# A delta-rule chain between two feed-forward layers: one tiling for K S and Q S, and a fixed place for each step of a chunk

## The chip, the cores and the metric

The kernel runs on one core of a Trainium2 chip. The metric is the device time of one execution in microseconds. A core has five engines, each with an instruction queue of its own that it works through in order: TensorE (PE, with its weight loads as PEld), VectorE (DVE), ScalarE (ACT), GpSimd (POOL) and SyncE (SP), which here issues the DMAs. They meet only through semaphores.

## The reference

A recurrence over 768 tokens for 32 pairs of batch and head (state 48 x 48), then two feed-forward layers over the 3072 tokens, 384 to 2048 to 384 each, all in float32:

```python
for t in range(S):
    kt, vt, bt = (k_n[:, :, t], v[:, :, t], beta[:, :, t, None])
    y[:, :, t] = np.einsum('bhd,bhde->bhe', q[:, :, t], state)
    v_old = np.einsum('bhde,bhd->bhe', state, kt)
    state = state + bt[:, :, :, None] * np.einsum('bhd,bhe->bhde', kt, vt - v_old)
...
g = np.where(pos, h, np.where(neg, 0.0, (h + beta) ** 2 / (4.0 * beta)))   # layer 1, h = x @ w_in
...
r = np.maximum(h, 0.0); g = r * r                                            # layer 2
```

Here k_n is k divided by its norm. Each layer ends with g @ w_out.

## The kernel before

**Chunks.** The 768 tokens are cut into 24 chunks of 32 tokens. A chunk has the 4 batches x 32 tokens on 128 partitions and the 8 heads side by side. For chunk c the steps are, all as short matmuls on tiles of TensorE's array: `ks` (K S and Q S from the state `st` into the two tiles `yo`, line 507; L516 on VectorE, twice, makes the residual `r` from it), `tr` (the triangular inverse times the residual, line 521, copied out by L529 on ScalarE), `ku` (K'U, line 556, into two tiles `sps`; four additions L568 on VectorE bring it into the state), `pu` (P U added to Q S in `yo`, line 538; L546 on ScalarE and L547 on VectorE write y) and `xt` (three transposes, line 585; L587 on ScalarE and L588 on VectorE split the result into `xh` and `xl`, the input of the first feed-forward layer). The state makes `ks` of a chunk wait for `ku` of the one before.

**Tiles of K S.** `kqt` holds k and q of a chunk side by side (2 x 32 columns). For chunks from 4 on, the loads swap k and q for odd batches, so one matmul of 64 columns puts K S and Q S of every batch where they belong. Chunks 2 and 3 (0 and 1 don't use the state) are loaded unswapped: there a matmul of 64 columns serves the even batches and two of 32 columns the odd ones, in turn. The profile shows each float32 matmul as two.

**Grams and solves.** `gram(c)` makes the products of a chunk's k and q (line 301, masked by L317). The chunks stand in groups (2, 4, 4, 4, 4, 4, 2); for each group one triangular solve `tri` turns the grams into inverses: L371 transposes on VectorE, some small steps lead up to L410, 30 pairs of L431 and L432 run on GpSimd, and L435 transposes back on VectorE. GpSimd also scales each chunk's v (L277).

**Feed-forward.** The tokens go through layer 1 in nine blocks of 2 or 3 chunks (SIZES 2, 2, 3, 3, 3, 3, 3, 2, 3), then through layer 2 in eight of 3 chunks. A block takes 16 iterations f. In iteration x TensorE does `hidden` (h, 9 matmuls, line 602) and, two iterations late, `out1` or `out2` (acc, 9 matmuls, line 602). Between them ScalarE and VectorE work in turn: L628, L629, L630, L631, L639, L640 in layer 1. Weights for layer 2 are converted on the way (L186, L189, L195).

**Order.** TensorE's order is the program's; that of the other engines comes from a scheduler. An iteration has two slots: slot 2x stands behind `hidden`, slot 2x+1 behind the output products. A block has 32 slots. Block n's chunks run in the slots of block n-1 (those of block 1 from slot 19 on). Before, the five steps of a block's chunks, with the grams of the next group put between the steps of one chunk, stood in one list that was spread evenly over the slots. `ready` and `at`, the slots of grams and of `ks`, set when the solves begin and end: L371 one slot after the group's last gram, L435 one slot ahead of the `ks` of the group's first chunk.

Of the kernel before, what the change touches and what calls it, by code (L numbers as in the profile page):

```python
# [19 lines left out]
SIZES = [2, 2, 3, 3, 3, 3, 3, 2, 3]  # L20

GROUPS = [2, 4, 4, 4, 4, 4, 2]
# [3 lines left out]
def kernel(  # L26
# [25 lines left out]
    B, H, T = 4, 8, 32  # L52
# [16 lines left out]
    KQ, KG = 4, 2  # L69
# [3 lines left out]
    HEAD = 19  # L73
# [214 lines left out]
    def gram(c, lo=0, hi=2, late=0, eng=None):  # L288


        n, j = group_of[c]
        if j == 0 and lo == 0:
            gp[n] = ring.tile([P, 2, GC, H, T], F32, tag="gp", bufs=2, name="gp")
            if GROUPS[n] < GC:
                nc.gpsimd.memset(gp[n][:, 0, GROUPS[n]:], 0.0)
        g = att([P, H, hi - lo, T], "g")
        src = kqt[c] if c < KQ else kqg[c]

        def one_(b, h, p, pd):
            x = src[pd, b // 2, h]  # L300
            nc.tensor.matmul(  # L301
                g[p, h].rearrange("p x i -> p (x i)"), x[:, 0:T], x[:, lo * T:hi * T],
                start=h == 0, stop=True, skip_group_check=True,
            )

        per_bh(one_)
        if c >= KQ:
            kqg.pop(c)
            if late < 2:
                load_kg(c + KG)  # L310

        dst = gp[n][:, lo:hi, j].rearrange("p x h i -> p h x i")
        if late > 1:
            nc.scalar.copy(dst, g)

        def keep():
            (eng or nc.vector).tensor_mul(  # L317
                dst,
                dst if late > 1 else g,
                mask[:, lo:hi].rearrange("p (o x) i -> p o x i", o=1)  # L320
                .to_broadcast([P, H, hi - lo, T]),
            )

        if late:
            return keep
        keep()
# [151 lines left out]
    def chunk_steps(c):  # L478
        n, j = block_of[c]
        g, gj = group_of[c]  # L480
        t = {}

        def of_heads(o, x):

            for a in range(c):
                per_bh(lambda b, h, p, pd: nc.tensor.matmul(
                    o[p, h], cross[a, c][p, h, x], us[a][p, h],
                    start=a == 0 and h == 0, stop=x == 0 and a == c - 1,
                    skip_group_check=True,
                ))  # L490

        def ks():
            r = t["r"] = kvt[c][:, 1]
            if 0 < c < HEADS:
                o = att([P, H, D], "ks")
                of_heads(o, 0)
                nc.vector.tensor_sub(r, r, o)
            elif c:
                o = t["o"] = [ps.tile([P, H, D], F32, tag=f"yo{x}", name="yo") for x in range(2)]

                def one_(b, h, p, pd):
                    x = kqt[c][pd, b // 2, h]
                    rows = [(x, 64 * (b // 2), 64)]
                    if b % 2 and c < KQ:
                        rows = [(x[:, 0:T], T * b, T), (x[:, T:2 * T], T * (b - 1), T)]
                    for x, q, w in rows:
                        nc.tensor.matmul(  # L507
                            o[b % 2][q:q + w, h], x, st[pd, b // 2, h],
                            start=h == 0, stop=False, skip_group_check=True,
                        )  # L510

                per_bh(one_)
                kqt.pop(c)
                load_kq(c + KQ)
                for x in range(2):
                    nc.vector.scalar_tensor_tensor(  # L516
                        r, o[x], side[:, 2 * x:2 * x + 1], r, ALU.mult, ALU.add)

        def tr():
            o = att([P, H, D], "tr")  # L520
            per_bh(lambda b, h, p, pd: nc.tensor.matmul(  # L521
                o[p, h], gp[g][p, 0, gj, h], t["r"][p, h],
                start=h == 0, stop=True, skip_group_check=True,
            ))
            if c >= HEADS:
                us[c] = t["r"]
            else:
                us[c] = wp.tile([P, H, D], F32, tag=spare[f"u{c}"], name="u")
            nc.scalar.copy(us[c], o)  # L529

        def qs():
            o = t["o"] = att([P, H, D], "yy")
            of_heads(o, 1)

        def pu():
            o = t["o"]
            y = t["y"] = t["r"]
            per_bh(lambda b, h, p, pd: nc.tensor.matmul(  # L538
                o[p, h] if c < HEADS else o[b % 2][T * (b ^ 1):T * (b ^ 1) + T, h],
                gp[g][p, 1, gj, h], us[c][p, h],  # L540
                start=c == 0 and h == 0, stop=True, skip_group_check=True,
            ))
            if c < HEADS:
                nc.scalar.copy(y, o)
            else:
                nc.scalar.mul(y, o[0], side[:, 1:2])  # L546
                nc.vector.scalar_tensor_tensor(y, o[1], side[:, 3:4], y, ALU.mult, ALU.add)  # L547

        def ku():
            k_ = kvt[c]  # L550
            if c < NCH - 1:
                kf = k_.rearrange("p x h d -> p (x h d)")
                w = 64 if c == 0 else D
                if c not in range(1, HEADS):
                    s_ps[:] = [att([P, H, D], "sps") for x in range(B2)]
                per_bh(lambda b, h, p, pd: nc.tensor.matmul(  # L556
                    s_ps[b // 2][pd.start:pd.start + w, h], kf[p, D * h:D * h + w], us[c][p, h],
                    start=c not in range(1, HEADS) and h == 0, stop=c >= HEADS - 1,
                    skip_group_check=True,
                ))  # L560
                if c == HEADS - 1:
                    nc.vector.tensor_copy(st[:, 0], s_ps[0])
                    nc.scalar.copy(st[:, 1], s_ps[1])
                elif c >= HEADS:
                    for x in range(B2):
                        for o in range(2):
                            d = st[64 * o:64 * o + D, x]
                            nc.vector.tensor_add(d, d, s_ps[x][64 * o:64 * o + D])  # L568
            done()

        def done():

            t["n"] = t.get("n", 0) + 1
            if t["n"] == 2:
                del kvt[c]
                load_kv(c + 3)

        def xt():
            if j == 0:
                xh[n] = ring.tile([P, KT, P * SIZES[n]], F32R, tag="xh", bufs=2, name="xh")  # L580
                xl[n] = ring.tile([P, KT, P * SIZES[n]], F32R, tag="xl", bufs=2, name="xl")
            o = att([P, KT, P], "xt")
            yf = t["y"].rearrange("p h d -> p (h d)")
            for kt in range(KT):
                nc.tensor.transpose(o[:, kt], yf[:, kt * P:(kt + 1) * P], ident)
            cols = slice(j * P, (j + 1) * P)
            nc.scalar.copy(xh[n][:, :, cols], o)  # L587
            marks[2] = nc.vector.tensor_sub(xl[n][:, :, cols], o, xh[n].bitcast(F32)[:, :, cols])  # L588
            done()

        if c < HEADS:
            return [ks, tr, qs, pu, ku, xt]
        return [ks, tr, ku, pu, xt]
# [189 lines left out]
    with tc.manual_schedule(engines=ENGINES):  # L783
# [32 lines left out]
        def put_a(n, slot, f):  # L816
            exa.setdefault(SL * n + slot, []).append(f)
# [5 lines left out]
        for i, c in enumerate(range(GFIRST[2], GFIRST[3])):  # L823
            ready[c] = 4 + 3 * i
            put_a(0, ready[c], lambda c=c: gram(c))
        for n in range(1, NB):
            todo = []
            for c in range(FIRST[n], FIRST[n] + SIZES[n]):
                g, j = group_of[c]
                due = []  # L830
                if j == 0 and 2 <= g < NG - 1:
                    due = list(range(GFIRST[g + 1], GFIRST[g + 1] + GROUPS[g + 1]))
                for i, s_ in enumerate(chunk_steps(c)):
                    todo.append(((at, c) if i == 0 else None, s_))
                    if i and due:
                        x = due.pop(0)
                        todo.append(((ready, x), lambda x=x: gram(x)))
                assert not due
            for i, (mark, s_) in enumerate(todo):
                o = 0 if n > 1 else HEAD  # L840
                slot = SL * (n - 1) + o + i * (SL - o) // len(todo)
                if mark:
                    mark[0][mark[1]] = slot
                put_a(0, slot, s_)
        put(0, HEAD - 1, *later(end1))
        for c in range(HEADS):
            put(0, 8 + 4 * c, lambda c=c: load_kq(c + KQ))
# [116 lines left out]
```

## Time and profile before

| | us |
|---|---|
| median of three runs | 1078.85 (1078.58 to 1081.9) |
| profiled execution | 1083.08 |
| its span, first to last instruction | 1081.3 |
| TensorE busy | 997.5 (92%) |
| VectorE busy | 643.0 (59%) |
| ScalarE busy | 474.2 (44%) |
| GpSimd busy | 309.9 (29%) |

Rows of the timeline give the start of a piece of work and its length; names are those of the code above, `<-` stands between what is written and what is read, and xN is the count of instructions. "Idle" is the time in which the engine stood still just before, with what ended it. PEclk is the granted TensorE clock as a share of 2.4 GHz. A busy TensorE isn't TensorE at its peak: a slow clock and drained tiles count as busy.

### The profile page before, as it was taken

The numbers are of one execution on the slowest core, as the hardware profiler recorded it, in microseconds if no ns is written. First come the engines' busy times: TensorE is split into PE (matmuls) and PEld (weight loads), VectorE is DVE, ScalarE is ACT, GpSimd is POOL, SyncE is SP. The second block draws the span as 40 slices with busy tenths as digits, with TensorE's granted clock in tenths as the row PEclk, the third lists the DMA queues.
The fourth block names the chain that finished last, engine by engine and source line by source line (L and its number), as shares of the span: only waits on it lengthen the run. The fifth ranks groups of instructions, "written<-read, shape, count | busy, mean of one in ns | idle before, by whom it ended". The sixth has DMA issues, their size and how long they took to land.

```text
span 1081.3 us, 30535 instructions
## 1 busy us (share of the span) xinstructions
PE 997.5 (92%) x13096; PEld 952.3 (88%) x13096; DVE 643.0 (59%) x1168; ACT 474.2 (44%) x974; POOL 309.9 (29%) x465
## 2 busy tenths in 40 slices
PE   4448989989999999899999999999999999999997
PEld 4437878979888898889999999999999999999996
DVE  6986648677676767767757678643434343443332
ACT  2684326445453554454454564433333333333332
POOL 3890570086008504813920113110101010010000
PEclk9967889989999999999999999999999999999999
DMA  9773125343262352431102133110101010000000
GB/s 263 216 215 106 31 59 173 96 117 107 74 174 57 97 148 61 133 97 32 56 27 76 38 111 106 41 45 1 45 1 45 1 45 1 23 1 23 1 23 22
DMA packets 67174, 80.71 MB, mean 75 GB/s; under 512 B 36640, under 2 KB 50464, under 8 KB 67040
## 3 DMA queue, kind: packets, MB, share of 16 engines
q1 hardware_dynamic: 67040, 78.78, 25.6%
q8 instruction: 102, 1.67, 0.7%
q14 instruction: 32, 0.26, 0.1%
HBM read 63.03 MB, written 15.73 MB: 73 GB/s over the span
## 4 chain that ended last, share of the span: by engine, by line
PE 75%; DVE 11%; DMA 6%; ACT 4%; issue 2%; SPq 0%; DVEq 0%; ACTq 0%
PE h L602 33%; PE acc L602 33%; DMA raw<-in_w_dram 5%; PE yo L507 3%; PE tr L521 2%; DVE g L631 2%; PE g L301 1%; DVE gl L640 1%; DVE g L629 1%; PE sps L556 1%; DVE st L568 1%; DVE kv L516 1%; ACT r L628 1%; PE yo L538 1%; DVE wl L195 1%
## 5 line engine op out<-in xcount | busy, mean ns | idle before, releaser
L602 PE MATMUL h<-xh,w 128*128 128x384 f32 (+1 forms) x1632 | 322.9, 334 | 5.0 <-ACT r L628 4.4
L602 PEld LDWEIGHTS h<-xh,w 128*128 128x128 f32 x1632 | 275.9, 192 | 9.6 <-ACT r L628 5.2
L640 DVE TENSOR_TENSOR gl<-g,gh 128x384 fp32r<-128x384 f32 (+1 forms) x272 | 166.1, 611 | 124.4 <-ACT gh L639 118.9
L639 ACT CAST gh<-g 128x384 fp32r<-128x384 f32 (+1 forms) x272 | 134.5, 494 | 191.1 <-DVE g L631 82.3
L602 PE MATMUL h<-xl,w 128*128 128x384 f32 (+1 forms) x816 | 180.5, 330 | 0.0
L602 PE MATMUL acc<-gh,w 128*128 128x384 f32 (+1 forms) x864 | 168.3, 331 | 2.3 <-ACT gh L639 1.4
L634 DVE TENSOR_TENSOR g<-r 128x384 f32<-128x384 f32 x128 | 71.3, 557 | 158.1 <-ACT r L633 158.1
L602 PE MATMUL acc<-w,gh 128*128 128x384 f32 x768 | 156.4, 339 | 1.9 <-DVE e L647 1.9
L633 ACT ACTIVATE r<-h,zero 128x384 f32<-128x384 f32 x128 | 74.5, 582 | 167.2 <-PE h L602 167.2
L602 PEld LDWEIGHTS acc<-gh,w 128*128 128x128 f32 x864 | 139.0, 193 | 6.9 <-ACT gh L639 1.9
L602 PEld LDWEIGHTS h<-xl,w 128*128 128x128 f32 x816 | 142.7, 192 | 0.0
L602 PEld LDWEIGHTS acc<-w,gh 128*128 128x128 f32 x768 | 137.0, 188 | 2.2 <-ACT gh L639 2.2
L628 ACT ACTIVATE r<-h,one 128x384 f32<-128x384 f32 (+1 forms) x144 | 78.3, 544 | 109.6 <-PE h L602 108.9
L431 POOL TENSOR_TENSOR t<-tx,gm 128x30 f32<-128x30 f32 (+9 forms) x180 | 109.2, 607 | 18.5 <-DVE tx L410 4.9
L432 POOL TENSOR_TENSOR tx<-tx,t 128x30 f32<-128x30 f32 (+9 forms) x180 | 106.6, 592 | 17.6 <-DVE tx L411 4.0
L631 DVE SCALAR_TENSOR_TENSOR g<-r,g 128x384 f32<-128x384 f32 (+1 forms) x144 | 83.7, 581 | 42.0 <-ACT g L630 40.0
L630 ACT ACTIVATE g<-g 128x384 f32<-128x384 f32 (+1 forms) x144 | 70.3, 488 | 71.0 <-DVE g L629 70.2
L629 DVE TENSOR_SCALAR g<-r 128x384 f32<-128x384 f32 (+1 forms) x144 | 64.4, 448 | 54.7 <-ACT r L628 53.4
L693 POOL CAST xh<-x2r 128x1152 fp32r<-128x1152 f32 x8 | 9.4, 1173 | 293.8 <-PE h L602 293.7
L602 PE MATMUL acc<-gl,w 128*128 128x384 f32 (+1 forms) x432 | 92.2, 323 | 1.5 <-DVE gl L640 1.5
L602 PE MATMUL acc<-w,gl 128*128 128x384 f32 x384 | 88.5, 338 | 0.0
L277 POOL TENSOR_TENSOR kv<-kv,nt 128x384 f32<-128x384 f32 x24 | 21.2, 883 | 189.4 <-DMA kv<-in_kv_dram 75.8
(99 smaller groups left out, 949.1 us busy)
## 6 DMA issues: line engine op xcount, KB each, us to landing
raw<-in_w_dram SPq DMA_DIRECT2D x64, 384.0 KB, 3.7
kqt<-in_kq_dram SPq DMA_DIRECT2D x68, 192.0 KB, 3.9
kv<-in_kv_dram SPq DMA_DIRECT2D x24, 384.0 KB, 3.2
w2f<-wl SPq DMA_DIRECT2D x32, 192.0 KB, 3.1
w2r<-w2f SPq DMA_DIRECT2D x16, 384.0 KB, 3.0
x2r<-x SPq DMA_DIRECT2D x8, 576.0 KB, 4.3
out_dram<-e SPq DMA_DIRECT2D x88, 48.0 KB, 1.6
kqt<-in_kq_dram SPq DMA_DIRECT2D x40, 96.0 KB, 3.6
```

The costliest lines, as they stand in the source:

```text
L431: eng.tensor_mul(t, by.to_broadcast(shape), of.to_broadcast(shape))
L432: eng.tensor_add(rest, rest, t)
L507: nc.tensor.matmul(o[b % 2][q:q + w, h], x, st[pd, b // 2, h], start=h == 0, stop=False, skip_group_check=True,)
L602: nc.tensor.matmul(o, *((r, l) if swap else (l, r)), **flags)
L628: marks[0] = nc.scalar.activation(r, h, AF.Relu, bias=one)
L629: marks[1] = nc.vector.tensor_scalar(g, r, 2.0, 0.5, ALU.min, ALU.mult)
L630: nc.scalar.activation(g, g, AF.Square)
L631: nc.vector.scalar_tensor_tensor(g, r, -1.0, g, ALU.add, ALU.max)
L633: marks[0] = nc.scalar.activation(r, h, AF.Relu, bias=zero)
L634: marks[1] = nc.vector.tensor_mul(g, r, r)
L639: nc.scalar.copy(ghi, g)
L640: nc.vector.tensor_sub(glo, g, ghi.bitcast(F32))
```

## The change

In `ks`, chunks 2 and 3 now use two matmuls of 32 columns for every batch, even and odd. The list of steps is gone: each chunk has an equal share of the slots between its block's first slot and the next block's, and within its share `ks` stands at 0, `tr` at 0.36, `ku` with `pu` directly behind it at 0.62, and `xt` at 1.2, which is in the share of the next chunk, or at 0.94 for a block's last chunk. Grams of the next group stand at 0.5 and 0.82, two to a chunk, so that a group's four take two chunks.

```diff
-                    if b % 2 and c < KQ:
-                        rows = [(x[:, 0:T], T * b, T), (x[:, T:2 * T], T * (b - 1), T)]
+                    if c < KQ:
+                        rows = [(x[:, 0:T], T * b, T), (x[:, T:2 * T], T * (b ^ 1), T)]
...
+            o = 0 if n > 1 else HEAD
+            span = (SL - o) / SIZES[n]
+            for k, c in enumerate(range(FIRST[n], FIRST[n] + SIZES[n])):
...
+                    due += range(GFIRST[g + 1], GFIRST[g + 1] + GROUPS[g + 1])
+                last = k == SIZES[n] - 1
+                ks, tr, ku, pu, xt = chunk_steps(c)
...
+                    slot = SL * (n - 1) + o + int(span * (k + part))
...
+                at[c] = place(0, ks)
+                place(0.36, tr)
+                place(0.62, lambda ku=ku, pu=pu: (ku(), pu()))
+                place(0.94 if last else 1.2, xt)
+                for part in (0.5, 0.82):
+                    if due:
                         x = due.pop(0)
-                        todo.append(((ready, x), lambda x=x: gram(x)))
-                assert not due
-            for i, (mark, s_) in enumerate(todo):
-                o = 0 if n > 1 else HEAD
-                slot = SL * (n - 1) + o + i * (SL - o) // len(todo)
...
+                        ready[x] = place(part, lambda x=x: gram(x))
```

Three places in the orders of the engines. The first is TensorE in the feed-forward block 0, the end of chunk 3's `ks` (`yo`) and what follows it; - is before, + is now:

```order
-L507 MATMUL yo<-st,kqt 64x48
-L507 MATMUL yo<-st,kqt 32x48 x2
+L507 MATMUL yo<-st,kqt 32x48 x64
 L602 MATMUL h<-xh,w_1442 128x256 x6
 L602 MATMUL h<-xl,w_1442 128x256 x3
-L521 MATMUL tr<-kv,gp 32x48 x32
+L585 MATMUL xt<-ident,kv 128x128 x3
 L602 MATMUL acc_1347<-gh,w_1388 128x256 x2
```

The alternating run became one run of 64 matmuls of 32 columns, `tr` moved one slot on, and the `xt` of the chunk before moved in behind h.

The second is TensorE at the edge between blocks 0 and 1: the last iteration of block 0, and the first h of block 1 (weights `w_847`).

```order
 L602 MATMUL h<-xl,w_1645 128x256 x3
-L585 MATMUL xt<-ident,kv 128x128 x3
 L602 MATMUL acc_1347<-gh,w_1628 128x256 x2
 L602 MATMUL acc_1348<-gh,w_1628 128x256 x2
...
 L602 MATMUL acc_1349<-gl,w_1628 128x256
+L585 MATMUL xt<-ident,kv 128x128 x3
 L602 MATMUL h<-xh,w_847 128x256 x6
```

The last chunk's `xt` moved from ahead of the output products to directly ahead of the next block's first h. At all eight edges it now stands there.

The third is VectorE at the end of block 2, where the solve of group 3 ends (L435). Before:

```order
L629 TENSOR_SCALAR g<-r 128x384
L435 STREAM_TRANSPOSE gp<-tx 128x32x32
L631 SCALAR_TENSOR_TENSOR g<-r,g 128x384
L640 TENSOR_TENSOR gl<-g,gh 128x384
L629 TENSOR_SCALAR g<-r 128x384
```

And now:

```order
L629 TENSOR_SCALAR g<-r 128x384
L435 STREAM_TRANSPOSE gp<-tx 128x32x32
L631 SCALAR_TENSOR_TENSOR g<-r,g 128x384
L588 TENSOR_TENSOR xl<-xt,xh 128x3x128
L640 TENSOR_TENSOR gl<-g,gh 128x384
```

L588, the half of `xt` that VectorE makes, moved in behind L435. Between this solve's L371 and its L435 stand 11 rows of L629, one for each iteration, where 16 stood; in group 4 it is 11 for 13, in group 5 11 for 14.

## Rows read from the trace of the kernel before

**Rows 1.** The page: busy time, share of the span and instructions of each engine.

```profile
PE 997.5 (92%) x13096; PEld 952.3 (88%) x13096; DVE 643.0 (59%) x1168; ACT 474.2 (44%) x974; POOL 309.9 (29%) x465
```

**Rows 2.** TensorE's waits: who waited for whom, us in total, times, longest.

```profile
PE tr L521 <- DVE kv L516: 11.7, 9, 2.3
PE xt L585 <- DVE kv L547: 8.2, 9, 1.6
...
PE tr L521 <- DVE tx L411: 3.5, 1, 3.5
```

**Rows 3.** TensorE's timeline around chunks 2, 3 and 5: start us, length us, work.

```profile
111.76 9.37 PE L507 MATMUL yo<-st,kqt 48*64 48x48 f32 x96
121.06 1.65 PE L602 MATMUL h<-xh,w 128*128 128x256 f32 x6
...
124.71 1.00 PE L602 MATMUL acc<-gh,w 128*128 128x256 f32 x6
...
132.69 9.61 PE L507 MATMUL yo<-st,kqt 48*64 48x48 f32 x96
...
173.79 0.87 PE L602 MATMUL h<-xh,w 128*128 128x256 f32 x6
...
174.93 0.88 PE L521 MATMUL tr<-kv,gp 32*32 32x48 f32 x64
175.75 0.97 PE L602 MATMUL acc<-gh,w 128*128 128x256 f32 x6
```

**Rows 4.** Short matmuls in unbroken runs: two groups by shape, one timeline row.

```profile
L507 PE MATMUL yo<-st,kqt 48*64 48x48 f32 x64 | 1.1, 220 | 0.0
...
L301 PE MATMUL g<-kqt 48*32 48x64 f32 x64 | 1.1, 218 | 0.0
...
112.00 0.28 PE L507 MATMUL yo<-st,kqt 48*32 48x48 f32 x4
```

**Rows 5.** By stretch: length, busy PE, PEld, DVE, ACT, POOL, then PEclk, DMA, GB/s.

```profile
112.00:122.00 10.00, 10.00 (x100) 7.28 (x99) 5.10 (x10) 0.82 (x2) 3.51 (x7) 0.63 0.00 0
```

**Rows 6.** VectorE's timeline beside chunk 2's K S.

```profile
115.23 0.75 DVE L410 TENSOR_TENSOR tx<-gm,st 128x512 f32<-128x512 f32 x1
120.87 0.62 DVE L516 SCALAR_TENSOR_TENSOR kv<-yo,side,kv 128x384 f32<-128x384 f32 x1 [4.90 <-PE yo L507]
...
121.82 0.61 DVE L516 SCALAR_TENSOR_TENSOR kv<-yo,side,kv 128x384 f32<-128x384 f32 x1
```

**Rows 7.** TensorE's timeline from tr to sps, chunks 7 and 8.

```profile
220.92 1.50 PE L521 MATMUL tr<-kv,gp 32*32 32x48 f32 x64 [3.52 <-DVE tx L411]
...
227.39 0.93 PE L556 MATMUL sps<-kv 32*48 32x48 f32 x64
...
244.94 0.88 PE L521 MATMUL tr<-kv,gp 32*32 32x48 f32 x64 [0.62 <-DVE kv L516]
...
249.07 0.93 PE L556 MATMUL sps<-kv 32*48 32x48 f32 x64
```

**Rows 8.** TensorE's timeline at the first block's start.

```profile
66.61 0.90 PE L585 MATMUL xt<-ident,kv 128*128 128x128 f32 x3 [4.32 <-ACT kv L544]
68.08 1.65 PE L602 MATMUL h<-xh,w 128*128 128x256 f32 x6 [0.57 <-ACT xh L587]
```

**Rows 9.** VectorE's and GpSimd's timelines: solves of groups 3 and 5.

```profile
212.50 2.15 DVE L371 STREAM_TRANSPOSE gm<-gp 128x1024 f32<-128x1024 f32 x1
...
262.30 0.27 POOL L432 TENSOR_TENSOR tx<-tx,t 128x30 f32<-128x30 f32 x1
...
282.34 2.22 DVE L435 STREAM_TRANSPOSE gp<-tx 128x1024 f32<-128x1024 f32 x1
...
412.83 2.24 DVE L371 STREAM_TRANSPOSE gm<-gp 128x1024 f32<-128x1024 f32 x1
...
460.86 0.28 POOL L432 TENSOR_TENSOR tx<-tx,t 128x30 f32<-128x30 f32 x1
```

**Rows 10.** VectorE's longest wait from 284 to 362.5 us.

```profile
DVE g L629 <- ACT r L628: 11.2, 9, 2.9
```

More of the change, by code (lines that the diff above doesn't have):

```diff
@@ L825, with place @@
             put_a(0, ready[c], lambda c=c: gram(c))
+        due = []
         for n in range(1, NB):
-            todo = []
-            for c in range(FIRST[n], FIRST[n] + SIZES[n]):
+            o = 0 if n > 1 else HEAD
+            span = (SL - o) / SIZES[n]
+            for k, c in enumerate(range(FIRST[n], FIRST[n] + SIZES[n])):
                 g, j = group_of[c]
-                due = []
                 if j == 0 and 2 <= g < NG - 1:
[L832 to L835, printed above, removed]
-                        x = due.pop(0)
-                        todo.append(((ready, x), lambda x=x: gram(x)))
-                assert not due
-            for i, (mark, s_) in enumerate(todo):
-                o = 0 if n > 1 else HEAD
-                slot = SL * (n - 1) + o + i * (SL - o) // len(todo)
-                if mark:
-                    mark[0][mark[1]] = slot
-                put_a(0, slot, s_)
+                    due += range(GFIRST[g + 1], GFIRST[g + 1] + GROUPS[g + 1])
+                last = k == SIZES[n] - 1
+                ks, tr, ku, pu, xt = chunk_steps(c)
+                def place(part, f):
+                    slot = SL * (n - 1) + o + int(span * (k + part))
+                    put_a(0, slot, f)
+                    return slot
+                at[c] = place(0, ks)
[4 more added lines that the diff above has]
+                    if due:
+                        x = due.pop(0)
+                        ready[x] = place(part, lambda x=x: gram(x))
         put(0, HEAD - 1, *later(end1))
```

## The prediction

> **What bounds the kernel now.** I read the page first, for the engines: TensorE is busy 92% of the span, VectorE 59%, and no other engine comes near [rows 1]. So a saving counts only if it takes time from TensorE's own row of work: matmuls that take long, or waits. The waits of TensorE come next. Of its idle time behind the first 150 us nearly all stands in front of two steps of the chunk recurrence: the product tr waits for VectorE's L516 (11.7 us in nine waits) and once for work queued ahead of that (3.5 us), and the transposes xt wait for L547 (8.2 us in nine waits) [rows 2]. Then TensorE's row in order of time, around the first chunks that use the state. Chunk 2's K S and Q S take 9.37 us for 96 matmuls, and chunk 3's 9.61 us [rows 3]. The same step of a later chunk, 64 matmuls on one tiling, takes 1.1 us [rows 4]. The reader is to see that these two stretches count as busy while little is done in them: their granted clock is 0.63 [rows 5], the level of 1.2 GHz for most of the stretch, and what follows still runs at that level. Behind some 610 us only feed-forward work is left, which the change doesn't touch.
>
> **One: K S and Q S of chunks 2 and 3.** Before, matmuls of 64 columns and of 32 columns alternate, 32 times in 9.4 us; a run of four of one kind starts within 0.28 us, and the time goes between the kinds [rows 3, 4]. After, 128 matmuls of 32 columns stand in a row. Their price is not in the trace. The nearest row is the gram of a chunk, the same 48 x 32 tiles in an unbroken run: 1.1 us for 64 [rows 4], so 2.2 us for 128. Bounds: 1.8 us by tr's 0.88 us for 64 tiles of 32 x 32 [rows 3], and 9.0 us if runs of four never overlapped (32 times 0.28). I take 2.2 and save 9.37 + 9.61 - 4.4 = 14.6 us. The clock gives more: h and tr behind chunk 2's step took 3.65 us (121.06 to 124.71), and at the full clock 1.96 us (173.79 to 175.75) [rows 3], 1.7 us each for two chunks, 3.4. One part comes back. In the 9.4 us VectorE caught up with the first triangular solves: L410 ends at 115.98, and the two L516 with what stands between take 1.56 us (120.87 to 122.43), so chunk 2's residual is ready at about 117.6 [rows 6]. TensorE would reach tr at 111.76 + 2.2 + two half iterations of 1.14 (173.79 to 174.93) = 116.3 and waits some 1.2 us. Sum of part one: 14.6 + 3.4 - 1.2 = **16.8 us**, bounds 1 and 17.5.
>
> The Trainium skill (TensorE: Matmul & The Clock Gate, Part 3, "The mechanism") states a rule against this part: a weight load overlaps running matmuls only when it goes to another row group. After the change four instructions in a row use one row half, before only the pairs of one column tile. If each load then stood alone, the part would gain little or lose; the run of four in 0.28 us [rows 4] speaks against it. What that would give is the last rival below.
>
> **Two: the waits in front of tr and xt.** K S to tr was one or two half iterations and is three or four; P U to xt was one or two and is four to six, since xt of a chunk stands behind the next chunk's K S. A half iteration is 1.7 us ((4.13 - 0.82) / 2, from tr at 244.94 to sps at 249.07, less tr itself) [rows 3, 7], and the longest wait for L516 was 2.3 us, so these waits go: 11.7 + 3.5 + 8.2 = 23.4 us. The 3.5 us wait had also dropped the clock: tr, acc and h behind it took 6.47 us (220.92 to 227.39) instead of 4.13 [rows 7], so 2.3 us more. I leave 1.5 us of waits standing. Gain 24.2 us; bounds 20 and 25.7. K'U and P U in one slot I cost at nothing: L568 and L547 then stand together on VectorE, 2.9 us, but the next h takes 1.7 us of it and P U 0.8.
>
> **Three: the edge between blocks.** The last chunk's xt now stands directly ahead of the next block's first h, which reads what xt makes; before, at least one half iteration lay between. The only such pair in the trace: xt at 66.61, h at 68.08, 0.57 us waited for ScalarE's L587 [rows 8]. There are eight edges. One belongs to part four. Of the others, two also have the solve's transpose L371 (2.2 us [rows 9]) on VectorE ahead of L588; these I price at 2.2, the other five between 0.57 and 1.2, with ScalarE's queue, at 0.9. Cost 5 x 0.9 + 2 x 2.2 = 8.9 us; bounds 4 and 12.
>
> **Four: the solves of groups 3, 4 and 5.** The grams of a group now spread over two chunks, so its solve begins later, and its end L435 stays ahead of the next group's first chunk. In VectorE's order 11 iterations (rows of L629) stand between L371 and L435 where 16, 13 and 14 stood. GpSimd needs from L371 to its last L432 50.1 us (212.50 to 262.57) in group 3 and 48.3 us in group 5 (412.83 to 461.14) [rows 9]. VectorE reached L435 69.84 us after L371 in group 3 (to 282.34), over 16 iterations with 5.8 us of wait and slow clock in them [rows 7, 9]: 4.0 us an iteration. Eleven take 44 us. So L435 waits for GpSimd, about 6, 5 and, with an edge in its window, 3 us, where before GpSimd was done 20 us ahead in group 3. VectorE runs its queue in order. In group 3 the last xl (L588) of the block stands behind L435, and the next block's first h waits for it: 6 us and 1 us for the edge, then a slower clock as in [rows 7], 2.3: 9.3 us. In groups 4 and 5 what waits behind L435 is L631 and L640 of the running iteration, and TensorE has about 2 us more than L435's own 2.2 us before it runs out of work: 3 and 1 us. Cost **13.3 us**; bounds 0 (TensorE loses the time elsewhere, and GpSimd is never late) and 22 (6 + 1 + 5 + 3, and the clock drops each time).
>
> **The sum.** Part two to four: 24.2 - 8.9 - 13.3 = +2.0 us. With part one 18.8 us. The profiled execution took 1083.08 us (span 1081.3), so 1064.3 us; it lies 4.2 us above the median of the three runs, 1078.85, and I carry the difference over: **1060 us**.
>
> **The rivals.** (a) *The waits go and nothing replaces them.* GpSimd is on time within 1 us and the edges cost 4 to 5 us: 16.8 + 24.2 - 5 - 1 = 35 us, 1044 us. For it: margins of 20 us in group 3 before; against it: 11 iterations cannot hold 48 us unless TensorE waits. (b) *VectorE is the next bound.* In block 3 (284 to 362.5 us) VectorE waited for new h only 11.2 us of 78.5 [rows 10]; once TensorE's waits are gone and L435 blocks it, the iterations lag. Then 5 us of waits stay instead of 1.5, and part four costs its upper end 22: 24.2 - 3.5 - 8.9 - 22 = -10, the sum 6.6, 1072 us. (c) *Part one gains little*: the 128 matmuls take some 9 us each time, the sum is 18.8 - 13.6 = 5 less the clock's 3.4: 2 us, 1077 us. (d) *Slower*: the matmuls in one row half do not overlap, and each costs what each of the 96 did, 98 ns: 12.5 us for 128, 6 us more over both chunks than before, the clock stays low, tr doesn't wait. With part two to four at +2 that is 4 us slower, 1083 us. It decides from about 90 ns a matmul on; 17 ns is what the gram's row gives.
>
> **How the numbers follow.** Forecast 0.57 (1053 to 1068), (a) 0.17, (b) 0.17, (c) 0.05, (d) 0.04. About 0.3%, 3.2 us, is what a measurement of this kernel can tell from no change. Faster: 0.57 + 0.17 + 0.17 = 0.91, the same 0.05, slower 0.04. The range leaves out (c), (d) and the outer third of (a) and of (b), 0.20 in all, and so holds their centres with some of the bounds of parts three and four: 1043 to 1074.
>
> **What would show it.** Right: L507 of chunks 2 and 3 at 2 to 3 us for 128 and the clock at full behind it; TensorE's waits for L516 and L547 gone; new waits of h for L587 or L588 at block edges; the longest wait of TensorE at the edge where group 3's L435 stands, and GpSimd's last L432 directly ahead of L435 in groups 3 to 5. Wrong: L507 at 9 us or more (part one); L435 starting well behind the last L432 (part four); or tr still waiting for L516, which would mean VectorE lags by more than three half iterations.

## The result, and the profile after

The median went from 1080.13 to 1071.05 us: ratio 0.9915, 95% interval 0.9892 to 0.9937. In what follows a ratio less 1 is put against 1080 us, so that runs of different sets can be compared: the change makes the kernel **9.2 us faster** (6.8 to 11.7), where 18.8 was forecast. The profiled execution took 1071.74 us, the one of before 1083.08.

The page of the changed kernel, span, engines and the chain that ended last:

```profile
span 1070.0 us, 30658 instructions
...
PE 983.0 (92%) x13160; PEld 944.6 (88%) x13160; DVE 648.6 (61%) x1168; ACT 471.9 (44%) x974; POOL 311.1 (29%) x465
...
PE 67%; DVE 11%; POOL 8%; DMA 6%; issue 3%; ACT 3%; SPq 0%; DVEq 0%; ACTq 0%; POOLq 0%
```

TensorE is 14.5 us less busy than in [rows 1], over a span only 11.3 us shorter. GpSimd, which had no share of the chain before, now has 8% of it, all from the solves (L431, L432).

TensorE's waits from 100 to 700 us (total, times, longest), to be laid beside [rows 2]:

```profile
PE h L602 <- ACT xh L587: 12.1, 8, 3.3
PE h L602 <- ACT r L628: 8.4, 6, 3.1
PE h L602 <- DVE xl L588: 3.7, 3, 3.3
...
PE tr L521 <- DVE kv L516: 1.8, 1, 1.8
...
PE xt L585 <- DVE kv L547: 0.6, 1, 0.6
```

Of the 23.4 us in front of tr and xt 2.4 are left. In their place h waits at the edges between blocks, for the halves of xt (L587, L588), which in this window it didn't do before.

TensorE's timeline around chunks 2 and 3, which answers to [rows 3]:

```profile
113.96 1.38 PE L507 MATMUL yo<-st,kqt 48*32 48x48 f32 x128
...
119.85 0.88 PE L521 MATMUL tr<-kv,gp 32*32 32x48 f32 x64 [1.79 <-DVE kv L516]
120.67 1.36 PE L602 MATMUL h<-xh,w 128*128 128x256 f32 x6
```

K S and Q S take 1.38 us for 128 matmuls, 10.8 ns each, less than the 2.2 us I had taken. Behind the wait of tr the clock still falls for a moment: h takes 1.36 us, and the two steps of h and acc behind tr 3.84 us (120.67 to 124.51), some 1.5 more than the same steps five microseconds later.

TensorE at the worst edge, block 2 to 3, and VectorE and ScalarE there; the last row is a stretch (length, busy PE, PEld, DVE, ACT, POOL, then PEclk):

```profile
264.86 2.29 PE L602 MATMUL h<-xh,w 128*128 128x384 f32 x6 [2.94 <-ACT xh L587]
270.42 1.33 PE L602 MATMUL h<-xl,w 128*128 128x384 f32 x3 [3.27 <-DVE xl L588]
271.68 1.96 PE L507 MATMUL yo<-st,kqt 48*64 48x48 f32 x64
...
257.68 2.24 DVE L568 TENSOR_TENSOR st<-st,sps 48x384 f32<-48x384 f32 x4
259.95 0.62 DVE L547 SCALAR_TENSOR_TENSOR kv<-yo,side,kv 128x384 f32<-128x384 f32 x1
260.48 0.39 DVE L629 TENSOR_SCALAR g<-r 128x384 f32<-128x384 f32 x1
...
263.26 0.63 DVE L629 TENSOR_SCALAR g<-r 128x384 f32<-128x384 f32 x1
267.43 2.06 DVE L435 STREAM_TRANSPOSE gp<-tx 128x1024 f32<-128x1024 f32 x1 [3.54 <-POOL tx L432]
...
269.83 0.54 DVE L588 TENSOR_TENSOR xl<-xt,xh 128x384 fp32r<-128x384 f32 x1
...
260.90 0.53 ACT L630 ACTIVATE g<-g 128x384 f32<-128x384 f32 x1 [3.13 <-DVE g L629]
...
264.35 0.46 ACT L587 CAST xh<-xt 128x384 fp32r<-128x384 f32 x1
...
262.00:278.00 16.00, 9.87 (x87) 8.83 (x88) 7.38 (x12) 4.79 (x10) 5.31 (x13) 0.58 0.28 75
```

Here two costs stand one behind the other. First L568 and L547 in a row (2.9 us) make L629 late; ScalarE stands 3.13 us in front of its L630, and L587 comes only behind that iteration and the next one's L630, so h waits 2.94 us for the first half of xt. Then VectorE stands 3.54 us in front of L435 until GpSimd's last L432 is done, with L588 queued behind it, and h waits 3.27 us more. The granted clock of these 16 us is 0.58, the level of 1.2 GHz for most of it: from 270.42 to 278.32 us TensorE does what takes it some 4.4 us at the full clock (xl 0.52, K S 1.08, acc 1.65, h 1.14, by starts of the same work around it).

Three more edges, blocks 3 to 4, 4 to 5 and 7 to 8, with the solve's transpose L371 that stands at the second of them:

```profile
344.53 1.32 PE L602 MATMUL h<-xh,w 128*128 128x384 f32 x6 [2.69 <-ACT xh L587]
...
416.10 2.14 DVE L371 STREAM_TRANSPOSE gm<-gp 128x1024 f32<-128x1024 f32 x1
...
417.63 1.31 PE L602 MATMUL h<-xh,w 128*128 128x384 f32 x6 [0.57 <-ACT xh L587]
...
602.73 2.29 PE L602 MATMUL h<-xh,w 128*128 128x384 f32 x6 [3.29 <-ACT xh L587]
```

The ends of the solves of groups 4 and 5, VectorE's timeline:

```profile
368.75 2.20 DVE L435 STREAM_TRANSPOSE gp<-tx 128x1024 f32<-128x1024 f32 x1 [3.02 <-POOL tx L432]
...
465.63 2.18 DVE L435 STREAM_TRANSPOSE gp<-tx 128x1024 f32<-128x1024 f32 x1 [1.69 <-POOL tx L432]
```

### The profile page after: what moved, and what is told of

Same layout as the page of the kernel before. It is cut to its first block, busy times and chain, and to the rows that moved or that the text cites. A ratio compares the mean times of both kernels' runs of the same rounds, so it can differ in the third digit from the quotient of the medians.

```text
span 1070.0 us, 30658 instructions
## 1 busy us (share of the span) xinstructions
PE 983.0 (92%) x13160; PEld 944.6 (88%) x13160; DVE 648.6 (61%) x1168; ACT 471.9 (44%) x974; POOL 311.1 (29%) x465
## 3 DMA queue, kind: packets, MB, share of 16 engines
q8 instruction: 103, 1.69, 0.7%
## 4 chain that ended last, share of the span: by engine, by line
PE 67%; DVE 11%; POOL 8%; DMA 6%; issue 3%; ACT 3%; SPq 0%; DVEq 0%; ACTq 0%; POOLq 0%
PE h L602 31%; PE acc L602 30%; DMA raw<-in_w_dram 6%; POOL t L431 4%; POOL tx L432 4%; DVE gl L640 2%; DVE g L629 1%; DVE g L631 1%; PE yo L507 1%; PE sps L556 1%; DVE st L568 1%; PE tr L521 1%; PE g L301 1%; PE yo L538 1%; ACT gh L639 1%
## 5 line engine op out<-in xcount | busy, mean ns | idle before, releaser
L602 PE MATMUL h<-xh,w 128*128 128x384 f32 (+1 forms) x1632 | 325.7, 336 | 21.4 <-ACT xh L587 12.7
L602 PE MATMUL acc<-gh,w 128*128 128x384 f32 (+1 forms) x864 | 165.7, 328 | 3.8 <-ACT gh L639 2.4
L431 POOL TENSOR_TENSOR t<-tx,gm 128x30 f32<-128x30 f32 (+9 forms) x180 | 110.0, 611 | 17.6 <-DVE tx L410 4.3
L631 DVE SCALAR_TENSOR_TENSOR g<-r,g 128x384 f32<-128x384 f32 (+1 forms) x144 | 88.1, 612 | 39.1 <-ACT g L630 37.8
L432 POOL TENSOR_TENSOR tx<-tx,t 128x30 f32<-128x30 f32 (+9 forms) x180 | 106.5, 592 | 13.9
L630 ACT ACTIVATE g<-g 128x384 f32<-128x384 f32 (+1 forms) x144 | 70.2, 488 | 86.8 <-DVE g L629 86.3
L628 ACT ACTIVATE r<-h,one 128x384 f32<-128x384 f32 (+1 forms) x144 | 78.3, 543 | 67.1 <-PE h L602 66.5
L629 DVE TENSOR_SCALAR g<-r 128x384 f32<-128x384 f32 (+1 forms) x144 | 66.0, 459 | 35.9 <-ACT r L628 35.0
```

What stands on the lines that cost most here:

```text
L431: eng.tensor_mul(t, by.to_broadcast(shape), of.to_broadcast(shape))
L432: eng.tensor_add(rest, rest, t)
L602: nc.tensor.matmul(o, *((r, l) if swap else (l, r)), **flags)
L628: marks[0] = nc.scalar.activation(r, h, AF.Relu, bias=one)
L629: marks[1] = nc.vector.tensor_scalar(g, r, 2.0, 0.5, ALU.min, ALU.mult)
L630: nc.scalar.activation(g, g, AF.Square)
```

## The experiments

Ratios are against the kernel before, in the same set of runs.

| run | what it is | ratio (95%) | us by 1080 |
|---|---|---|---|
| changed kernel | | 0.9915 (0.9892 to 0.9937) | -9.2 |
| e1_tiles | tiles alone | 0.9918 (0.9891 to 0.9945) | -8.9 |
| e2_steps | places of the steps alone | 1.0044 (1.0022 to 1.0066) | +4.8 |
| e3_edge | changed, last xt a slot or two earlier | 0.9843 (0.981 to 0.9875) | -17.0 |
| e4_grams | changed, four grams in one chunk | 0.9877 (0.9831 to 0.9923) | -13.3 |
| e5_both | e3 and e4 together | 0.9777 (0.9744 to 0.9811) | -24.1 |
| e6_apart | changed, P U apart from K'U | 0.9963 (0.9945 to 0.9981) | -4.0 |
| e7_twice | before, K S of chunks 2, 3 issued twice | 1.0225 (1.0191 to 1.0259) | +24.3 |
| e8_tr | e5, chunk 2's tr a slot later | 0.9779 (0.974 to 0.9817) | -23.9 |
| e9_next | e5, P U in the slot behind K'U | 0.9731 (0.9681 to 0.9781) | **-29.1** |

**The two halves of the change.** e1 is the kernel before with the edit of the tiles; e2 the changed kernel without it.

```diff
-                    if b % 2 and c < KQ:
-                        rows = [(x[:, 0:T], T * b, T), (x[:, T:2 * T], T * (b - 1), T)]
+                    if c < KQ:
+                        rows = [(x[:, 0:T], T * b, T), (x[:, T:2 * T], T * (b ^ 1), T)]
```

> The kernel before with the K S edit alone: chunks 2 and 3 in 32-column tiles, the old list of steps. Theory A (the edit of the tiles is worth about 15 us, and the new places of the steps lose about as much as they gain, or some 4 us more): 14 to 17 us faster than before, 1063 to 1067 us, so faster than the changed kernel (1071); L507 of chunks 2 and 3 at 1.4 to 2.2 us; TensorE's waits of tr for L516 and of xt for L547 still at some 11 and 8 us. Theory B (the tiles give half of that, because VectorE and the solve of group 2 are late in their place, and the steps give nothing): 7 to 10 us faster, 1070 to 1073 us.

> The changed kernel with the old K S tiles (64 and 32 columns in turn) in chunks 2 and 3: the new places of the steps alone. Theory A: 1081 to 1087 us, not faster than before, with L507 of chunks 2 and 3 at 9 us each, no waits of tr for L516 left, and new waits of h for L587 of some 10 us. Theory B: 1078 to 1080 us.

The tiles alone bring 8.9 us (5.9 to 11.8), the steps alone cost 4.8 (2.4 to 7.1), and the whole brings 9.2. So the halves don't add (8.9 - 4.8 = 4.1): on top of the new places the tiles are worth 9.2 + 4.8 = 14.0 us, some 3 us either way. TensorE's timeline of e1 shows where its gain goes in the old order, and the waits from 100 to 200 us, of e1 and then of before (second profile, b2_before), show how much:

```profile
112.46 1.38 PE L507 MATMUL yo<-st,kqt 48*32 48x48 f32 x128
...
118.30 1.30 PE L521 MATMUL tr<-kv,gp 32*32 32x48 f32 x64 [3.24 <-DVE kv L516]
119.53 1.65 PE L602 MATMUL acc<-gh,w 128*128 128x256 f32 x6
```

```profile
PE tr L521 <- DVE kv L516: 5.8, 4, 3.2
...
PE xt L585 <- DVE kv L547: 3.3, 3, 1.7
```

```profile
PE tr L521 <- DVE kv L516: 2.4, 2, 1.2
PE xt L585 <- DVE kv L547: 2.2, 3, 1.0
```

The waits for L516 and L547 grow from 4.6 to 9.1 us: TensorE, no longer held up by its own K S, now runs into VectorE. In e2 these waits are gone (from 100 to 700 us 0.7 us at xt, none at tr), and the edges stand there instead. The profile is of an execution of 1079.39 us where e2's median is 1085.45, so it shows where the waits stand and not all that the median pays:

```profile
PE h L602 <- ACT xh L587: 11.4, 8, 3.3
...
PE h L602 <- DVE xl L588: 3.8, 3, 3.4
```

**What the alternating run costs.** e7 issues it twice in the kernel before; b2 is that kernel once more, for a second profile.

```diff
-                per_bh(one_)
+                [per_bh(one_) for _ in range(1 + (c < KQ))]
```

> The kernel before with the alternating K S and Q S of chunks 2 and 3 issued twice in a row (the second writes the same values again): 2 x 96 more matmuls, 64 changes of tiling more. It asks what one such run really costs in the median, since the tiling edit alone brought 8.5 us where I had counted 16.8. Theory A, the run costs what the profile showed, 9.4 and 9.6 us, and the edit's missing gain went elsewhere: 19 us more, and up to 3 us more for the clock: 1098 to 1103. Theory B, the profiled execution of before showed it dear and most executions pay less, 6 to 7 us a run: 1092 to 1095.

> The kernel before once more, for a second profile of it. Its first profiled execution took 1083.08 us, 2.6 above the median of its runs. Theory A (the alternating runs cost the same each time): L507 of chunks 2 and 3 at 9.2 to 9.6 us, and 43.5 to 45 us from chunk 2's K S to chunk 4's (44.2 before). Theory B (the first profile was a dear one): L507 at 8.2 us or less and 40 to 42 us between the two.

TensorE's L507 of chunks 2 and 3, of e7 and then of b2:

```profile
112.11 20.27 PE L507 MATMUL yo<-st,kqt 48*64 48x48 f32 x192
...
143.61 18.95 PE L507 MATMUL yo<-st,kqt 48*64 48x48 f32 x192
```

```profile
112.98 8.14 PE L507 MATMUL yo<-st,kqt 48*64 48x48 f32 x96
...
133.17 8.00 PE L507 MATMUL yo<-st,kqt 48*64 48x48 f32 x96
```

Two runs more cost 24.3 us (20.6 to 28.0), so the price in the profile is real in the time, and the theory that most executions pay less falls; the median is even above the first theory's range, and L507 takes 39.2 us in e7's profile, 23.1 more than in b2's. But the first profile was a dear one too: 18.98 us for the two runs, 16.14 in the second, which took 1079.65 us (with 42.3 us from chunk 2's K S to chunk 4's, just above the second theory's range). Adding two runs costs 24 us and taking both away gives back 9 to 14: what is added has no cover, what is taken away is capped by the next wait. With b2 as the base e1's gain can be counted out: L507 16.14 - 2.76 = 13.4; the full clock behind the two runs 3.4 (3.65 us twice against 1.96, as in [rows 3]); less 4.5 of new waits, 1.5 of slow clock behind the wait of tr (tr and acc start 3.45 us before sps, 1.95 at full clock) and a gap of 1.3 us in chunk 5's P U that the profile doesn't explain. Sum 9.5 us, and the two profiled spans differ by 1077.9 - 1068.4 = 9.5.

**Whether tr's place is the limit behind chunk 2.** e8 is e5 with chunk 2's tr behind the next h.

```diff
-                place(0.36, tr)
+                place(0.5 if c == HEADS else 0.36, tr)
```

> The changed kernel with both earlier edits (xt at 0.84, four grams in one chunk), and chunk 2's tr one slot later, behind the next h; VectorE's order is the same. It asks why the tiling edit gave half of what I counted. In the kernel without this last edit tr of chunk 2 waits 1.80 us for L516, which stands behind the end of another solve (L435, 2.19 us) on VectorE, and runs at the slow clock behind that wait. Theory A: the wait is a matter of TensorE's order; with h ahead of tr it goes, and with it the slow clock: 14.52 us from chunk 2's K S to chunk 3's become 11.5 to 12, the time 1056.8 becomes 1053 to 1055. Theory B: the chain from the solve over L516, tr, K'U and L568 to chunk 3's K S sets this stretch: tr starts no earlier, the wait turns up again at K'U or at chunk 3's K S, and the stretch stays at 14 to 14.8 us, the time at 1056 to 1058.

The median is 1057.0 us against e5's 1056.83: the second theory. TensorE's timeline of e8:

```profile
118.39 0.88 PE L521 MATMUL tr<-kv,gp 32*32 32x48 f32 x64
...
121.65 0.93 PE L556 MATMUL sps<-kv 32*48 32x48 f32 x64 [1.11 <-ACT kv L529]
```

The wait in front of tr is gone and the clock stays full behind it, but tr starts 5.98 us after K S (5.88 in e5), and TensorE waits at K'U instead. Chunk 3's K S begins 13.7 us after chunk 2's, between the two theories' numbers, but stands idle for 1.8 us within, which the profile ascribes to nothing, and from chunk 2's K S to chunk 4's it is 33.3 us against e5's 30.9. In both runs tr starts within 0.1 us of the end of the second L516 on VectorE, which stands behind the group's L435 there: an order of TensorE alone can't bring it forward.

**The edges.** e3 is the changed kernel with a block's last xt at 0.84 of its share.

```diff
-                place(0.94 if last else 1.2, xt)
+                place(0.84 if last else 1.2, xt)
```

> The changed kernel with a block's last xt at 0.84 of its share instead of 0.94, which is a slot of an even number (30 or 29 instead of 31): the output products then stand between it and the next block's first h. Theory A: TensorE's waits of h for L587 fall from 12.7 us to 1 to 3 us, the clock drops behind them go, 1061 to 1065 us. Rival (VectorE's queue is late there anyway, so TensorE loses the same time a little later at h for L628 or at the output products): 1068 to 1071 us.

-17.0 us instead of -9.2, as the first theory has it, and h's waits for L587 fall from 12.7 us in nine to 2.3 in three, over the whole run. What is left of group 3's edge is the solve:

```profile
268.38 1.33 PE L602 MATMUL h<-xl,w 128*128 128x384 f32 x3 [4.49 <-DVE xl L588]
```

**The late solves.** e4 is the changed kernel with the four grams of a group inside one chunk, e5 has both edits.

```diff
-                for part in (0.5, 0.82):
+                for part in (0.2, 0.5, 0.75, 0.87):
```

> The changed kernel with the four grams of the next group within one chunk again (at 0.2, 0.5, 0.75 and 0.87 of its share): the solves of groups 3 to 5 begin 10 to 11 slots earlier. Theory A: L435 waits for GpSimd in no group (3.5, 3.0 and 1.7 us in the changed kernel), the wait of h for L588 at the edge of block 2 (3.3 us) and those of h and acc behind L435 in groups 4 and 5 (4.5 us) go, 1063 to 1067 us. Rival (TensorE runs into VectorE's queue instead): 1069 to 1071 us.

> The changed kernel with both earlier edits at once: the last chunk's xt at 0.84 of its share instead of 0.94 (one or two slots ahead of the next block's first h), and the four grams of a group inside one chunk (0.2, 0.5, 0.75, 0.87), so that a solve begins 5 to 8 iterations earlier. Alone they gave about 6.6 and 3.6 us off the changed kernel's 1071.05. Theory A, edges and late solves are separate costs: the gains add, 1071 - 10 = 1061 us (1058 to 1063); no wait of h for L587 over 1 us, and GpSimd's last L432 well ahead of L435 in groups 3 to 5. Theory B, they are one cost, since the worst edge is the one at which group 3's solve ends: 1064 to 1066, as the moved xt alone.

In both no L435 waits for GpSimd any more. e3 brings 7.8 us over the changed kernel and both edits 14.9, so the grams bring 7.1 once xt is early. Alone, in e4, they bring 4.1, and this is not sure: its four runs lie at 1063 and at 1071 us, its interval overlaps with the changed kernel's, and in its profile, which is of a run at 1071.54, h waits longer for L587 than in the changed kernel (16.5 us for 12.1 from 100 to 700 us). So late solves and edges are two costs, but what is won at the one can be lost at the other. VectorE of e5 at group 3's L435, and the longest edge wait that is left:

```profile
262.63 2.19 DVE L435 STREAM_TRANSPOSE gp<-tx 128x1024 f32<-128x1024 f32 x1
...
478.82 2.29 PE L602 MATMUL h<-xh,w 128*128 128x384 f32 x6 [3.16 <-ACT xh L587]
```

**K'U and P U in one slot.** e6 takes them apart in the changed kernel, e9 in e5.

```diff
-                place(0.62, lambda ku=ku, pu=pu: (ku(), pu()))
+                place(0.62, ku)
+                place(0.76, pu)
```

```diff
-                place(0.62, lambda ku=ku, pu=pu: (ku(), pu()))
+                put_a(0, place(0.62, ku) + (n > 1), pu)
```

> The changed kernel with P U in a slot of its own again, at 0.76 of the chunk's share, one or two slots behind K'U at 0.62; xt stays where it is. Theory A: the long waits of h at block edges (2.9 and 3.3 us at block 3, 2.7 and 3.3 us at two others) come from K'U and P U in one slot, since four L568 and L547 then stand in a row on VectorE (2.9 us) and L629 and L630 behind them run late, so that ScalarE reaches L587 late. Then these waits fall to 0.6 to 1.2 us, h's waits for L587 and L588 from 16.4 us to 8 or 10, and the time to 1064 to 1067. Theory B: the edge waits come from xt alone standing ahead of h, whatever VectorE does before: the waits stay within 2 us of 16.4 and the time is 1070 to 1072.

> The changed kernel with both earlier edits, and from block 2 on P U in the slot behind K'U's instead of the same one, so that L629 comes between the four L568 and L547 on VectorE. With the solves late, P U one or two slots behind K'U had cost 8 us: L547 came to stand behind L435, and K S of the next chunk waited 5.6 us for it. Theory A: that was L435's fault; now that the solves end in time, no K S waits over 0.7 us for L547, the edge waits left (3.2 and 1.5 us for L587) shrink below 1, and the time goes from 1056.8 to 1052 to 1055. Theory B: K'U and P U in one slot cost nothing once the edges have a slot of room: 1056 to 1058. Theory C: K S waits for L547 at each chunk anyway, since it writes the two tiles that L547 reads: 1060 to 1066.

e6 is slower than the changed kernel by 5.2 us, which neither theory had. Its waits from 100 to 700 us say why:

```profile
PE yo L507 <- DVE kv L547: 8.6, 5, 5.6
...
PE h L602 <- ACT xh L587: 4.8, 8, 0.8
```

The long waits for L587 are gone, as the first theory has it (longest 0.8 for 3.3; those for L588 stay, 4.6 us). Not all of that is won: at the edge of block 2 to 3 xt itself now waits for L547, which P U's later place has made later,

```profile
266.29 0.55 PE L585 MATMUL xt<-ident,kv 128*128 128x128 f32 x3 [2.08 <-DVE kv L547]
```

and the 3.29 us at the last edge went for another reason (L629 no longer meets L696 there, see the last section). The greater loss is at K S: that of the next chunk writes the two tiles that L547 reads, and L547 had come to stand behind a late L435. VectorE of e6:

```profile
369.45 2.03 DVE L435 STREAM_TRANSPOSE gp<-tx 128x1024 f32<-128x1024 f32 x1 [3.53 <-POOL tx L432]
371.32 0.56 DVE L631 SCALAR_TENSOR_TENSOR g<-r,g 128x384 f32<-128x384 f32 x1
371.91 0.62 DVE L547 SCALAR_TENSOR_TENSOR kv<-yo,side,kv 128x384 f32<-128x384 f32 x1
```

With the solves in time the same separation pays: e9's median is 1050.29 us, 5.0 us below e5 by the ratios, and from 100 to 700 us TensorE waits for no L587 that its list shows. The intervals of e5 and e9 overlap (0.9744 to 0.9781), so the times alone don't settle it. The profiles help: the edit acts from chunk 4 on, and from chunk 4's K S to the end e9 takes 907.7 us, e5 914.7 and e8 912.7. So the step is worth about 5 to 7 us, by one profile each. e9 is the fastest version, 29.1 us (23.7 to 34.5) below the kernel before. What it waits for now is again xt and tr:

```profile
PE xt L585 <- DVE kv L547: 6.2, 4, 2.1
PE tr L521 <- DVE kv L516: 3.7, 2, 1.9
```

## Why the prediction was wrong

The sign and most of the named waits came out, and the time lay in the stated range; the gain was half of what I forecast. By the two halves, forecast against measured: part one 16.8, and on top of the new places 14.0, some 3 us either way; parts two to four +2.0, and by e2 **-4.8** (-7.1 to -2.4). So some 2.8 of the missing 9.6 us belong to part one, where they are within the noise, and 6.8 to the others, where they are not.

**Part one: mechanism right, size near.** The matmuls cost less than taken (1.38 us for 2.2, below my lower bound of 1.8) and the clock came back. I sized L507 by one dear execution, 18.98 us, where the second shows 16.14. The wait of tr for L516 was foreseen at 1.2 and is 1.79, with a slow clock behind it that I hadn't counted. The 16.8 held only for the new order; I worked tr's wait with two half iterations between K S and tr, which the old order doesn't have, and so didn't see that the tiles alone give 8.9. The rival that the matmuls in one row half don't overlap is out: 10.8 ns each against the 90 from which it decides. The Trainium skill's rule behind it (TensorE: Matmul & The Clock Gate, Part 3, "The mechanism") doesn't bind here: four loads in a row go to one row half, and all 128 matmuls take 1.38 us with their loads. Another page of the Trainium skill says that a change of tiling mode drains TensorE (TensorEngine Tiling (Array Packing), "Key Properties"); the trace agrees, as e7's 192 alternating matmuls take 19 to 20 us where 128 on one tiling take 1.4.

**Part two: the waits right.** 21.0 us of waits went, for 21.9 forecast, and the slow clock behind the 3.5 us wait with them.

**Part two's zero: the step that failed.** "K'U and P U in one slot I cost at nothing": the cover I named, the next h and P U, hides L568 and L547 from TensorE at that place, but on VectorE they delay L629, and with it L630 on ScalarE and all that ScalarE has behind it. In the changed kernel's rows this stands at three places: L629 starts 2.7, 1.8 and 2.7 us after the L628 that it reads has ended (at 260.48, 339.25 and 460.71 us), and h then waits 2.94 and 2.69 us for L587 where the undisturbed edges show 0.57, and 0.77 us for L628 within a block. My estimate from these rows is 2.4 + 2.1 + 0.8 = 5.3 us, most of the 6.8. e6 takes the long waits for L587 away but loses more at L547, and e9, with the solves in time, wins about 5 to 7 us by the same separation.

**Part three: the sum near by luck, 8.9 forecast and 9.6 us of waits found.** The total agrees, its terms don't. The two edges with L371, priced at 2.2, cost 0.8 each: L371 delays only L588, which h needs last, and 0.23 us of that is left in front of its second half. The edge of block 3 to 4, priced at 0.9, cost 2.69 by the zero above. The last, priced at 0.9, cost 3.29 with a slow clock behind (some 1.4 us): VectorE's L629 stands still there beside GpSimd (last section), which no term of mine had. The other three cost 0.57 to 0.91, as priced. e3 gets 7.8 us back by an earlier xt.

**Part four: mechanism right, near in size.** The waits of L435 for GpSimd are 3.54, 3.02 and 1.69 us, about half of the 6, 5 and 3 that I worked out, but group 3's edge costs what I had for it: 2.94 + 3.27 us of waits and 3.5 of slow clock (7.9 us for 4.4), 9.7 for 9.3. Of that the 2.94 comes from the zero and not from the solve; I had 1 us there. Group 4 costs 0.99 + 0.58 = 1.6 (3 forecast); group 5 2.16 and a slow clock of 1.4, some 3.6 (1 forecast). That is 15 us for 13.3, and some 12 without the zero's share.

**Together.** Without the zero parts three and four cost by these rows about what I forecast; with it the rows of parts two to four come to 3 or 4 us lost where I had 2 to gain. Behind chunk 4's K S the changed kernel takes 926.4 us, before in its second profile 922.7, 3.7 us more.

**The rivals.** The case that VectorE is the next bound (1072 us) hits the number by luck and half of the mechanism: L435 blocks VectorE and the clock falls, but the waits in front of tr and xt don't stay, as it says. The case without replacement (1044) is close to what e9 reaches once the replacements are taken out, 1050.

## What to carry to other kernels

A wait that is taken off an engine's path goes to the next in line: price it with the order that the change makes and not the old one, and test the two halves of a change apart, since here they didn't add (8.9 and -4.8 gave 9.2). Work that is "hidden" is hidden for one reader; follow it through the queues of the other engines to the next place where somebody waits, here from L568 over L629 and L630 to L587. And size a term by two profiled executions: the same run of matmuls took 19.0 us in one and 16.1 in the other.

## What the runs showed of the hardware

An instruction of VectorE can stand still beside one of GpSimd. In the changed kernel, VectorE and GpSimd ahead of the last edge:

```profile
596.60 0.29 DVE L629 TENSOR_SCALAR g<-r 128x256 f32<-128x256 f32 x1 [0.16 <-ACT r L628]
...
599.17 2.69 DVE L629 TENSOR_SCALAR g<-r 128x256 f32<-128x256 f32 x1
...
599.05 2.66 POOL L696 TENSOR_TENSOR xl<-x2r,xh 128x1152 fp32r<-128x1152 f32 x1
```

The same L629 takes 0.29 us alone and 2.69 us where L696 has begun 0.12 us before it; it ends 0.15 us after L696. In the kernel before the pair stands there too (2.77 and 2.73 us) and TensorE doesn't wait for it; now xt stands directly ahead of h, and TensorE pays 3.29 us. The Trainium skill (SBUF — State Buffer, "Who interferes with whom") has a rule for this: the two engines share a pair of ports, and where VectorE works in one of its two-port modes, which a tensor_scalar can enter, the one that issues second is blocked for the whole instruction of the other. The trace agrees: L629, the second to start, ends just behind L696. The mode itself no run shows.

The clock can stay low well beyond a wait: behind the two waits of 2.94 and 3.27 us the granted clock was 0.52 over the next 7.9 us (270.42 to 278.32), and 3.5 us went by it, more than either wait.
